# Weights decoded two chunks at a time, with loads, adds and the first batches placed anew, in an attention and FFN kernel

## Chip, cores and metric
One core of a Trainium2 chip. The metric is the device time of one execution in microseconds. All eight batches of an attention with memories and the FFN behind it run in one program; the host only lays arrays out.

## What is computed
Per batch and head, 32 memories gather keys and values of 576 positions with softmax weights over the heads' memory axis; queries attend to the 32 memories; the 4608 x 512 result goes through an FFN with a squared relu and d_ff = 2048. Inputs are fp32.

```
a = exp(phi - max(phi)); a = a / (sum(a) + 1e-9)
k_m = einsum('bhsm,bhsd->bhmd', a, k)
v_m = einsum('bhsm,bhsd->bhmd', a, v)
scores = q @ k_m.T / sqrt(64)
attn = exp(scores - max(scores)); attn = attn / (sum(attn) + 1e-9)
x = attn @ v_m, heads side by side
return square(relu(x @ w_in)) @ w_out
```

## The kernel before
**Names.** P = 128. A batch b has two tiles t of T = 288 tokens. d_ff is cut into 16 chunks f of 128. A *step* is one chunk f of one tile: `ffn1` (six matmuls on L566 into the PSUM tile h, relu on ScalarE at L568, the square at L572 on ScalarE or L574 on VectorE) and `ffn2` (matmuls into four accumulators). `ffn2` of a step runs two steps after its `ffn1` (LEAD). 256 steps, each cut into two *half steps*; steps of several tiles of batches 0 and 1 come in the order `runs` sets (tile (0,0), (0,1), (1,0) with chunks 0 to 3 first, then (1,1) with 0 to 7, ...).

**Attention folded into the FFN.** `attend` makes the softmax weights a of a tile over 4 x 2 heads x 32 memories, split into two fp32r parts a_hi and a_lo (L418, L419). `make_u` multiplies a unit n of w_in (512 columns of d_ff) with a batch's value memories, into the single PSUM tile ps_m, and splits it into u_hi (ScalarE, L456) and u_lo (VectorE, L458): unit (b,n). So `ffn1` is a @ u in three products: a_hi u_hi, a_hi u_lo, a_lo u_hi. `memories` also needs ps_m for every batch but the first.

**Weights.** w_in and w_out arrive as 64-bit words, in loads of 128 x 512 words (512 KB): w_in in 8 chunks of two halves, w_out in 16 chunks. `decode` turns a load into fp32: on ScalarE L479 (tile tmp) and L482 (tile low), on VectorE L484, L486 (mask and shift) and L489, then the add L496 on the engine that the plan names. `decode_out` then splits the chunk into two fp32r parts (L553 on ScalarE, L555 on VectorE); chunks 0 to 3 are first used whole in fp32 (L587, first 16 steps) and split later (`split_out`). Finished units of w_in are written to HBM (`keep_w`, L514) and streamed back for later batches. A load's tile is a `room` in the const pool; tmp has three buffers, low two.

**What sets the order.** The program is emitted in the order in which it should run; each engine takes its instructions in that order, and waits with everything behind. The start is written out: the list `loads` sets the order in which SP issues transfers (eight in flight), and the string `order` calls the generators of batch 0 (e exponentials, m memories, a0 and a1 the tiles' softmax, d0 to d3 the decodes of w_in chunks 0 and 1, u0 the first unit, s one filler matmul on ident). `spin` and `spin_r` are fillers whose results nobody reads; `spin_r` multiplies turn, a copy of e that L207 makes. After that the table `plan` gives each task of batches 0 to 2 and of the weights the half steps at which its parts are emitted; from batch 3 on a fixed pattern repeats. The dictionary in L945 drains some `ffn2` earlier than LEAD.

Of the kernel before, what the change touches and what calls it, by code (L numbers as in the profile page):

```python
# [24 lines left out]
def attn_moe_kernel(ctx: ExitStack, tc: tile.TileContext, qT, kv, phi, w_in, w_out, outT):  # L25
# [54 lines left out]
    def room(f, shape, dtype):  # L80
        return const.tile(shape, dtype, name=f"wo{f}")
# [97 lines left out]
    def exp_phi(b, e):  # L179
# [76 lines left out]
    def load_kv(b, qd, lent=None):  # L256

        got = []
        for c in range(NCH):
            if lent:  # L260
                t = lent(c)
            elif qd:

                name, bufs = ("tmp", 3) if c < 3 else ("low", 2)
                t = work.tile([P, 4, CW], F32, name=name, bufs=bufs)
            else:
                t = kvb[c]
                assert c not in kv_used
                kv_used.add(c)
# [106 lines left out]
    on_gpsimd = {(0, 0): (0, 1, 2), (0, 1): (0, 1, 2), (1, 0): (0, 1, 2), (1, 1): (0, 1), (2, 0): (1, 2), (2, 1): (0,)}  # L376

    def attend(b, t, q, mem, new_a):
# [18 lines left out]
        if starting:  # L397
            spin_r(*(turn[:, i:i + T] for i in (0, 1, 2, 4)))
# [65 lines left out]
    def fetch(src, f):  # L464
        raw = room(f, [P, src.shape[-1]], src.dtype)
        nc.sync.dma_start(out=raw, in_=src)
        return raw

    def decode(raw, new_out, adder):

        n = raw.shape[-1]

        def word(w, dtype):
            return raw.bitcast(dtype).rearrange("p (n w) -> p n w", w=2)[:, :, w]


        c = work.tile([P, n], I32, name="tmp", bufs=3)
# [3 lines left out]
        r = work.tile([P, n], I32, name="low", bufs=2)  # L481
# [17 lines left out]
    raws = {}  # L499
    w_in_at = {}  # L500


    lent = 2 * list(range(NFT - NQ * NFC, NFT))

    def fetch_w_in(n, qd):
        raws["in", n, qd] = fetch(w_in[n, qd], lent[NQ * n + qd])

    def fetch_w_out(f):
        raws["out", f] = fetch(w_out[f * P:(f + 1) * P], f)
# [7 lines left out]
    def decode_in(n, qd, adder=nc.gpsimd):  # L517

        def new_out():
            if n // 2 not in w_in_at:  # L520
                w_in_at[n // 2] = new_w()
            return w_in_at[n // 2][:, 2 * qd:2 * qd + 2, n % 2 * HC:n % 2 * HC + HC]

        yield from decode(raws.pop(("in", n, qd)), new_out, adder)
        ready.add(("in", n, qd))
# [7 lines left out]
    def decode_out(f, adder=nc.gpsimd, whole=False):  # L533

        def new_out():
            wo[f] = room(f, [P, DM], F32)
            return wo[f]

        w = yield from decode(raws.pop(("out", f)), new_out if whole else None, adder)
        if not whole:  # L540
            yield
            yield from split(f, w)
        ready.add(("out", f))

    def split_out(f):
        w = work.tile([P, DM], F32, name="tmp", bufs=3)
        nc.scalar.copy(w, wo[f])
        yield from split(f, w)

    def split(f, w):  # L550
        ready.discard(("out", f))
        wo[f] = room(f, [P, 2, DM], F32R)
        nc.scalar.copy(wo[f][:, 0], w)  # L553
        yield
        nc.vector.tensor_tensor(out=wo[f][:, 1], in0=w, in1=wo[f][:, 0].bitcast(F32), op=ALU.subtract)  # L555
        ready.add(("out", f))
# [68 lines left out]
    def new_mem(b):  # L625
        state[b]["mem"] = work.tile([P, 2, NPAIR, M], F32, name="mem", bufs=3)
# [44 lines left out]
    SQ_ACT = 39  # L671
# [52 lines left out]
    def next_kv():  # L724
# [36 lines left out]
    turn = const.tile([P, 3 * NQ * P], F32R, name=f"wo{NFT - 1}")  # L761
# [13 lines left out]
        "e e e e e m m d0 m m d0 s d0 a0 a0 a1 d1 d1 a0 a0 d1 u0 d2 a0 d2 u0 a0 u0 d3 d3 d2 s d3 s d3 a0"  # L775
# [11 lines left out]
    for n in kept:  # L787
# [5 lines left out]
        ((29, 29, 31), decode_in, 4, 0, nc.gpsimd),  # L793
        ((48, 53, 54), decode_in, 6, 0, nc.gpsimd),
        ((61,), task_kv, 2, 0),
        ((0, 1, 1), decode_out, 0, nc.gpsimd, True),
        ((6, 8, 10), decode_out, 3, nc.gpsimd, True),
        ((38, 43, 45), decode_in, 4, 1, nc.vector),
        ((110, 115), split_out, 0),
        ((5,), task_q, 1, 1),  # L800
        ((20,), fetch_w_in, 6, 1),
        ((90,), task_kv, 2, 1),
        ((0, 0, 2, 2, 3, 4), lambda: start["a1"]),
        ((50,), fetch_w_in, 7, 1),
        ((78, 81), split_out, 1),
        ((0, 1, 2), decode_out, 1, nc.gpsimd, True),
        ((47, 47, 49), decode_in, 6, 1, nc.vector),
        ((38,), fetch_w_out, 10),
        ((8,), fetch_w_in, 5, 0),
        ((62, 62, 64), decode_in, 7, 0, nc.vector),  # L810
        ((58, 59, 60), decode_in, 7, 1, nc.gpsimd),
        ((90,), task_stream, 2, 0),
        ((45, 46, 46, 48, 48), decode_out, 8, nc.vector),
        ((73, 73, 74), task_u, 0, 3),
        ((100, 101, 101, 102, 104, 107, 108), task_attend, 2, 0),
        ((52,), fetch_w_out, 13),
# [179 lines left out]
```

## Time and profile before

| | us |
|---|---|
| median of 3 runs | 739.28 |
| lowest, highest | 738.86, 742.27 |
| profiled execution | 739.42 |
| its span, first to last instruction | 737.6 |
| TensorE busy | 721.2 |
| VectorE, ScalarE, GpSimd busy | 379.6, 351.6, 263.8 |

The span is one execution on the core; 1.8 us lie around it. Times in the rows count from the span's start. TensorE's busy time is modelled at its ends, so a pause shorter than a matmul's tail does not show as idle; its weight loads (PEld) have rows of their own. A wait for several semaphores is put down to the one that came last.

### The profile page before, as it was taken

The page shows a single profiled execution, that of the slowest core. Times are in us where ns is not written, and L with a number is a line of the kernel's source. Part 1 is how long each engine was busy: PE and PEld are TensorE (multiplying, and loading weights), DVE is VectorE, ACT ScalarE, POOL GpSimd, SP SyncE. Part 2 cuts the span into 40 slices and gives each one's busy share as a digit, 9 for nine tenths or more (in the row PEclk, how much of TensorE's full clock was granted, in tenths as well). Part 3 has the DMA queues.
Part 4 walks back from the last instruction along what each step waited for, and adds up shares of the span by engine and source line. Part 5 has one row for each costly group of instructions (what it writes and reads, how often), then busy time and mean ns, then how long its engine had stood idle before and what let it go on. Part 6 is the DMA issues. An engine that isn't in the chain of part 4 may idle for free.

```text
span 737.6 us, 15709 instructions
## 1 busy us (share of the span) xinstructions
PE 721.2 (98%) x6170; PEld 655.1 (89%) x6170; DVE 379.6 (51%) x764; ACT 351.6 (48%) x750; POOL 263.8 (36%) x333
## 2 busy tenths in 40 slices
PE   8889999999999999999999999999999999999997
PEld 4467789889899898999899999899889999999997
DVE  4986779974565455254543556254542555321211
ACT  3546878874543344343544345433443435443332
POOL 1433334353443234332433324242333333333332
PEclk9999999999999999999999999999999999999999
DMA  9993228414429019131481216530391314100000
GB/s 306 354 363 117 105 67 265 147 30 125 140 76 313 25 56 298 44 122 34 143 222 44 80 33 244 122 121 2 87 281 31 122 34 147 58 33 1 33 2 32
DMA packets 64409, 89.61 MB, mean 121 GB/s; under 512 B 3984, under 2 KB 54928, under 8 KB 60752
## 3 DMA queue, kind: packets, MB, share of 16 engines
q1 hardware_dynamic: 63344, 87.34, 37.0%
q10 hardware_dynamic: 992, 1.28, 0.5%
q8 instruction: 48, 0.79, 0.4%
q14 instruction: 25, 0.20, 0.1%
HBM read 74.97 MB, written 13.63 MB: 120 GB/s over the span
## 4 chain that ended last, share of the span: by engine, by line
PE 83%; DVE 10%; ACT 4%; issue 1%; DMA 1%; POOL 1%; ACTq 0%; DVEq 0%; POOLq 0%
PE acc L595 49%; PE h L566 24%; PE ps_m L372 5%; PE ps_m L303 2%; DVE tmp L486 2%; DVE tmp L489 2%; PE acc L587 1%; DVE tmp L484 1%; DMA e_sb<-in_phi 1%; ACT low L482 1%; DVE u_lo L458 1%; ACT tmp L479 1%; DVE tmp L496 1%; ACT g L572 1%; ACT r L568 1%
## 5 line engine op out<-in xcount | busy, mean ns | idle before, releaser
L579 POOL TENSOR_TENSOR g_lo<-g,g_hi 128x288 fp32r<-128x288 f32 x240 | 202.4, 845 | 405.2 <-DVE g L574 313.3
L595 PE MATMUL acc<-g_hi,wo 128*128 128x288 f32 x1920 | 307.3, 298 | 0.4 <-DVE o L607 0.3
L595 PEld LDWEIGHTS acc<-g_hi,wo 128*128 128x128 f32 x1920 | 271.6, 188 | 25.3 <-ACT r L568 18.3
L574 DVE TENSOR_TENSOR g<-h,r 128x288 f32<-128x288 f32 x217 | 98.7, 456 | 307.3 <-ACT r L568 301.5
L568 ACT ACTIVATE r<-h 128x288 f32<-128x288 f32 x256 | 104.9, 410 | 295.0 <-PE h L566 286.4
L595 PE MATMUL acc<-g_lo,wo 128*128 128x288 f32 x960 | 176.5, 295 | 0.6 <-POOL g_lo L579 0.6
L595 PEld LDWEIGHTS acc<-g_lo,wo 128*128 128x128 f32 x960 | 144.2, 188 | 0.9 <-POOL g_lo L579 0.9
L577 ACT ACTIVATE g_hi<-r 128x288 fp32r<-128x288 f32 x240 | 106.5, 444 | 19.8 <-ACT r L568 0.8
L566 PE MATMUL h<-a_hi,u_hi 128*128 128x288 f32 x512 | 114.5, 305 | 0.7 <-ACT r L568 0.7
L566 PE MATMUL h<-a_hi,u_lo 128*128 128x288 f32 x512 | 109.8, 296 | 0.3 <-DVE u_lo L458 0.3
L566 PE MATMUL h<-a_lo,u_hi 128*128 128x288 f32 x512 | 109.6, 295 | 0.0
L566 PEld LDWEIGHTS h<-a_hi,u_hi 128*128 128x128 f32 x512 | 82.7, 188 | 10.5 <-issue 6.1
L566 PEld LDWEIGHTS h<-a_hi,u_lo 128*128 128x128 f32 x512 | 82.1, 188 | 0.5 <-DVE u_lo L458 0.5
L566 PEld LDWEIGHTS h<-a_lo,u_hi 128*128 128x128 f32 x512 | 82.2, 189 | 0.0
L458 DVE TENSOR_TENSOR u_lo<-ps_m,u_hi 128x1024 fp32r<-128x1024 f32 (+1 forms) x33 | 38.8, 1176 | 11.8 <-ACT u_hi L456 11.7
L372 PE MATMUL ps_m<-w_sb,mem 64*32 64x512 f32 (+1 forms) x528 | 37.1, 588 | 1.3 <-DVE w_sb L496 0.9
L587 PE MATMUL acc<-g_hi,wo 128*128 128x288 f32 x128 | 34.5, 414 | 1.7 <-POOL wo L496 1.7
L456 ACT CAST u_hi<-ps_m 128x1024 fp32r<-128x1024 f32 (+1 forms) x33 | 32.3, 980 | 5.0 <-PE ps_m L372 3.0
L587 PEld LDWEIGHTS acc<-g_hi,wo 128*128 128x128 f32 x128 | 23.6, 193 | 10.3 <-POOL wo L496 2.5
L482 ACT ACTIVATE low<-wo 128x512 int32<-128x512 uint32 x32 | 21.6, 674 | 8.6 <-DVE w_sb L496 4.4
L489 DVE SCALAR_TENSOR_TENSOR tmp<-wo,tmp 128x512 int32<-128x512 int32 x32 | 24.4, 761 | 1.1
L479 ACT ACTIVATE tmp<-wo 128x512 f32<-128x512 f32 x32 | 21.5, 672 | 4.4 <-DMA wo<-in_w_in 2.7
(136 smaller groups left out, 485.1 us busy)
## 6 DMA issues: line engine op xcount, KB each, us to landing
w_sb<-w_f SPq DMA_DIRECT2D x24, 1024.0 KB, 5.7
out_t<-o SPq DMA_DIRECT2D x62, 144.0 KB, 1.9
wo<-in_w_in SPq DMA_DIRECT2D x16, 512.0 KB, 8.3
wo<-in_w_out SPq DMA_DIRECT2D x16, 512.0 KB, 6.7
q_sb<-in_q SPq DMA_DIRECT2D x28, 288.0 KB, 3.4
kvb<-in_kv SPq DMA_DIRECT2D x28, 256.0 KB, 6.6
tmp<-in_kv SPq DMA_DIRECT2D x18, 256.0 KB, 6.0
w_f<-w_sb SPq DMA_DIRECT2D x4, 1024.0 KB, 7.6
```

Of the source, the lines that this page charges most:

```text
L372: nc.tensor.matmul(bank(out, half)[M * pr:M * (pr + 1), :y.shape[-1]], mem[hs, x, pr], y, start=True, stop=True)
L456: nc.scalar.copy(u_hi[:, :, n0:n1], ps[:, :, :n1 - n0])
L458: nc.vector.tensor_tensor(out=u_lo[:, :, n0:n1], in0=ps[:, :, :n1 - n0], in1=u_hi[:, :, n0:n1].bitcast(F32), op=ALU.subtract)
L482: nc.scalar.activation(r, word(0, U32), AF.Copy, scale=2.0 ** -29)
L489: nc.vector.scalar_tensor_tensor(out=c, in0=word(1, I32), scalar=-0x40000000, in1=c, op0=ALU.bitwise_and, op1=ALU.bitwise_or)
L566: nc.tensor.matmul(h[:, :T], u[:, qd, fs], x[:, qd], start=(i == 0), stop=(i == len(todo) - 1))
L568: nc.scalar.activation(r, h[:, :T], AF.Relu)
L574: nc.vector.tensor_tensor(out=g, in0=h[:, :T], in1=r, op=ALU.mult)
L577: nc.scalar.activation(g_hi, r, AF.Square)
L579: nc.gpsimd.tensor_tensor(out=g_lo, in0=g, in1=g_hi.bitcast(F32), op=ALU.subtract)
L587: nc.tensor.matmul(acc[e][:, :T], wo[f][:, e * P:(e + 1) * P], g_hi, start=first, stop=last)
L595: nc.tensor.matmul(acc[e][:, :T], wo[f][:, w, e * P:(e + 1) * P], x, start=first and x is g_hi and w == 0, stop=last and x is g_lo,)
```

## The change
`fetch` puts two loads of 512 KB side by side in one room, and `decode`, `decode_out` and `split` work on both at once, 128 x 1024; only w_in chunk 0 is still decoded by halves. The wide tmp has two buffers, the wide low one. Most adds are placed on VectorE: w_out pair 2 and w_in chunk 5 alone, and the two halves of w_in chunk 0, stay on GpSimd. Of the attention steps of batches 1 and 2 six of the operations 0 (subtract the maximum), 1 (multiply by the reciprocal) and 2 (a_lo) come from GpSimd to VectorE on balance. `spin_r` and the copy turn go; the start has plain fillers instead. SQ_ACT, the step up to which ScalarE makes the square, goes from 39 to 43. `loads`, `order`, `plan` and the early drains are new tables throughout.

```diff
-    def room(f, shape, dtype):
-        return const.tile(shape, dtype, name=f"wo{f}")
+    def room(k, shape, dtype):
+        return const.tile(shape, dtype, name=f"wp{k}")
...
-            nc.scalar.copy(turn.rearrange("p (c x) -> p c x", c=3), e_sb[:, :3])
...
-    on_gpsimd = {(0, 0): (0, 1, 2), (0, 1): (0, 1, 2), (1, 0): (0, 1, 2), (1, 1): (0, 1), (2, 0): (1, 2), (2, 1): (0,)}
+    on_gpsimd = {(0, 0): (0, 1, 2), (0, 1): (0, 1, 2), (1, 0): (), (1, 1): (), (2, 0): (2,), (2, 1): (2,)}
...
-            spin_r(*(turn[:, i:i + T] for i in (0, 1, 2, 4)))
+            spin(2, ident)
...
-    def fetch(src, f):
-        raw = room(f, [P, src.shape[-1]], src.dtype)
-        nc.sync.dma_start(out=raw, in_=src)
-        return raw
+    def fetch(src, key, k, i):
+        if key not in raws:
+            raws[key] = room(k, [P, 2, src.shape[-1]], src.dtype)
+        nc.sync.dma_start(out=raws[key][:, i], in_=src)
+        fetched.add((*key, i))
...
-        c = work.tile([P, n], I32, name="tmp", bufs=3)
+        c = work.tile([P, 2 * DM], I32, name="tmp", bufs=2)[:, :n]
...
-        r = work.tile([P, n], I32, name="low", bufs=2)
+        r = work.tile([P, 2 * DM], I32, name="low", bufs=1)[:, :n]
...
+    def split(k, w):
+        ready.difference_update(("out", 2 * k + i) for i in range(2))
+        y = room(k, [P, 2, 2, DM], F32R)
+        wo[2 * k:2 * k + 2] = [y[:, 0], y[:, 1]]
+        nc.scalar.copy(y[:, :, 0], w)
+        yield
+        nc.vector.tensor_tensor(out=y[:, :, 1], in0=w, in1=y[:, :, 0].bitcast(F32), op=ALU.subtract)
...
-    SQ_ACT = 39
+    SQ_ACT = 43
...
     loads = [
         (first_phi,),
         (first_kv, 0),
+        (task_q, 0, 1),
         (first_kv, 1),
-        (fetch_w_in, 0, 1),
         (fetch_w_in, 0, 0),
         (task_q, 0, 0),
-        (task_q, 0, 1),
+        (fetch_w_in, 0, 1),
         (fetch_w_in, 1, 0),
         (fetch_w_in, 1, 1),
+        (fetch_w_out, 2),
+        (next_kv,),
+        (fetch_w_in, 3, 1),
+        (fetch_w_out, 4),
         (fetch_w_out, 0),
         (fetch_w_out, 1),
...
-        ((0, 1, 1), decode_out, 0, nc.gpsimd, True),
-        ((0, 1, 2), decode_out, 1, nc.gpsimd, True),
+        ((0, 0, 0), decode_out, 0, nc.vector, True),
...
-        ((136, 142, 142), task_u, 2, 3),
-        ((109,), task_stream, 2, 3),
+        ((129, 134, 136), task_u, 2, 3),
+        ((112,), task_stream, 2, 3),
...
-        for _ in range({2: 1, 6: 1, 7: 1, 10: 1}.get(k, 0)):
+        for _ in range({2: 1, 7: 1, 8: 1, 9: 1}.get(k, 0)):
```

How the order moves at three places (line numbers in the second block of each are those of the changed file; names are out<-in with the shape of the output).

VectorE at the start, from the sum of tile (0,0)'s softmax to the u_lo of the first unit. Before:

```order
L406 TENSOR_REDUCE sm<-st 128x18
L407 TENSOR_SCALAR sm<-sm 128x18
L408 RECIPROCAL sm<-sm 128x18
L484 TENSOR_SCALAR tmp<-tmp 128x512
L486 TENSOR_SCALAR tmp<-tmp 128x512
L489 SCALAR_TENSOR_TENSOR tmp<-wo_129,tmp 128x512
L415 STREAM_TRANSPOSE at<-st 128x576
L458 TENSOR_TENSOR u_lo_333<-ps_m,u_hi_332 128x2x256
```

Now:

```order
L400 TENSOR_REDUCE sm<-st 128x18
L401 TENSOR_SCALAR sm<-sm 128x18
L402 RECIPROCAL sm<-sm 128x18
L478 TENSOR_SCALAR tmp<-tmp 128x1024
L480 TENSOR_SCALAR tmp<-tmp 128x1024
L483 SCALAR_TENSOR_TENSOR tmp<-wp_127,tmp 128x1024
L408 STREAM_TRANSPOSE at<-st 128x576
L490 ISA w_sb<-tmp,low 128x4x512
L451 TENSOR_TENSOR u_lo_344<-ps_m,u_hi_343 128x2x256
```

The decode of w_in chunk 1 between the reciprocal and the transpose is twice as wide, and its add stands ahead of u_lo.

ScalarE from the first FFN product's relu on. wo_133 and wo_391 are loads of w_out chunks 0 and 1; wp_373 is the room of both. Before:

```order
L568 ACTIVATE r<-h 128x288
L572 ACTIVATE g_hi<-r 128x288
L479 ACTIVATE tmp<-wo_133 128x512
L482 ACTIVATE low<-wo_133 128x512
L479 ACTIVATE tmp<-wo_391 128x512
L482 ACTIVATE low<-wo_391 128x512
L568 ACTIVATE r<-h 128x288
L572 ACTIVATE g_hi<-r 128x288
```

Now:

```order
L567 ACTIVATE r<-h 128x288
L571 ACTIVATE g_hi<-r 128x288
L473 ACTIVATE tmp<-wp_373 128x1024
L476 ACTIVATE low<-wp_373 128x1024
L449 CAST u_hi_343<-ps_m 128x2x256
L567 ACTIVATE r<-h 128x288
L571 ACTIVATE g_hi<-r 128x288
```

Four operations on halves become two on a pair, and the second half of the first unit's u_hi now stands behind them.

VectorE around the memories of batch 3, where u_lo of unit (2,3) frees ps_m and den is the first to read the memories. Before:

```order
L245 TENSOR_TENSOR e_sb<-e_sb,phi_mx 128x1024
L248 TENSOR_TENSOR e_sb<-e_sb,phi_mx 64x256
L574 TENSOR_TENSOR g<-h,r 128x288 x2
L458 TENSOR_TENSOR u_lo_3012<-ps_m,u_hi_3011 128x1024
L574 TENSOR_TENSOR g<-h,r 128x288
L312 TENSOR_SCALAR den<-ps_m 128x2
```

Now:

```order
L573 TENSOR_TENSOR g<-h,r 128x288 x2
L451 TENSOR_TENSOR u_lo_2704<-ps_m,u_hi_2703 128x1024
L224 STREAM_TRANSPOSE at<-phi_mx 128x256
L226 TENSOR_REDUCE top<-at 128x8
L229 TENSOR_TENSOR top<-top 32x8 x3
L231 COPY top<-top 32x8 x3
L573 TENSOR_TENSOR g<-h,r 128x288
L233 COPY at<-top 128x256
L234 STREAM_TRANSPOSE phi_mx<-at 128x256
L237 TENSOR_TENSOR e_sb<-e_sb,phi_mx 128x1024
L240 TENSOR_TENSOR e_sb<-e_sb,phi_mx 64x256
```

u_lo has moved ahead of all of batch 3's exponentials but their first maximum.

## Rows read from the trace of the kernel before

**Rows 1.** Section 1 of the page: busy time, share of the span and instructions of each engine.
```profile
PE 721.2 (98%) x6170; PEld 655.1 (89%) x6170; DVE 379.6 (51%) x764; ACT 351.6 (48%) x750; POOL 263.8 (36%) x333
```

**Rows 2.** Busy time by stretches; per engine busy us (x instructions), clock, DMA share, GB/s.
```profile
28.06:60.00 31.94, 26.65 (x261) 18.75 (x259) 25.86 (x42) 17.93 (x35) 11.73 (x10) 0.95 0.96 331
60.00:100.00 40.00, 39.35 (x233) 31.95 (x232) 30.00 (x46) 30.16 (x65) 15.05 (x12) 1.00 0.22 80
100.00:148.00 48.00, 47.35 (x377) 42.45 (x375) 41.96 (x64) 39.13 (x89) 19.91 (x20) 1.00 0.56 182
148.00:246.00 98.00, 95.95 (x872) 88.83 (x876) 57.76 (x113) 49.76 (x103) 39.08 (x54) 1.00 0.44 133
```

**Rows 3.** The chain of waits from 60 to 150 us, by line.
```profile
by line: DVE tmp L489 12.2%; DVE tmp L486 10.9%; DVE tmp L484 7.9%; ACT low L482 5.5%; ACT tmp L479 5.2%; issue 5.0%; DVE tmp L496 4.8%; ACT g L572 4.8%; ACT g_hi L577 4.3%; ACT r L568 4.1%; ACT wo L553 3.7%; DVE wo L555 3.4%; POOL tmp L496
```

**Rows 4.** The timeline before the first FFN product: start, us, engine, line [idle before <-releaser].
```profile
15.24 0.67 ACT L479 ACTIVATE tmp<-wo 128x512 f32<-128x512 f32 x1 [2.69 <-DMA wo<-in_w_in]
...
16.40 0.43 DVE L486 TENSOR_SCALAR tmp<-tmp 128x512 int32<-128x512 int32 x1
...
23.76 1.27 DVE L486 TENSOR_SCALAR tmp<-tmp 128x512 int32<-128x512 int32 x1
```

**Rows 5.** The timeline from the first FFN product to the third ffn2.
```profile
28.99 0.43 PE L566 MATMUL h<-a_lo,u_hi 128*128 128x288 f32 x2
...
36.26 2.21 PE L587 MATMUL acc<-g_hi,wo 128*128 128x288 f32 x8 [1.69 <-POOL wo L496]
...
40.28 1.37 DVE L174 TENSOR_TENSOR phi_mx<-at 128x256 f32<-128x256 f32 x1
...
42.15 0.57 PE L187 MATMUL ps_m<-ident,phi_mx 128*128 128x128 f32 x2 [2.37 <-DVE phi_mx L176]
...
48.27 1.50 DVE L484 TENSOR_SCALAR tmp<-tmp 128x512 f32<-128x512 f32 x1
...
50.80 2.21 PE L587 MATMUL acc<-g_hi,wo 128*128 128x288 f32 x8
```

**Rows 6.** Groups of one shape: xcount, busy us, mean ns, idle before; VectorE, ScalarE, then GpSimd.
```profile
L489 DVE SCALAR_TENSOR_TENSOR tmp<-wo,tmp 128x512 int32<-128x512 int32 x32 | 24.4, 761 | 1.1
L486 DVE TENSOR_SCALAR tmp<-tmp 128x512 int32<-128x512 int32 x32 | 22.3, 698 | 1.1
L484 DVE TENSOR_SCALAR tmp<-tmp 128x512 f32<-128x512 f32 x32 | 17.7, 554 | 1.1 <-ACT tmp L479 0.9
...
L412 DVE TENSOR_TENSOR st<-st,sm 128x576 f32<-128x576 f32 x11 | 8.3, 758 | 0.4
...
L496 DVE CUSTOM_DVE_ANT_0 w_sb<-tmp,low 128x1024 uint16<-128x1024 uint16 x9 | 7.2, 813 | 0.3
...
L210 DVE TENSOR_TENSOR e_sb<-e_sb,ps_m 128x1024 f32<-128x1024 f32 x2 | 2.4, 1217 | 1.9 <-PE ps_m L195 1.9
...
L479 ACT ACTIVATE tmp<-wo 128x512 f32<-128x512 f32 x32 | 21.5, 672 | 4.4 <-DMA wo<-in_w_in 2.7 <-DVE wo L555 1.7
...
L251 ACT ACTIVATE e_sb<-e_sb 128x1024 f32<-128x1024 f32 x5 | 5.2, 1044 | 0.0
...
L496 POOL TENSOR_TENSOR w_sb<-tmp,low 128x512 int32<-128x512 int32 x7 | 9.9, 1410 | 24.0 <-ACT tmp L479 14.2 <-ACT r L568 5.9 <-ACT o L614 2.7
```

**Rows 7.** DMAs issued at 4.8 to 5.0 and 26.2 to 26.4 us: KB each, us to landing.
```profile
wo<-in_kv SPq DMA_DIRECT2D x1, 128.0 KB, 7.8
...
wo<-in_w_out SPq DMA_DIRECT2D x1, 512.0 KB, 6.9
```

**Rows 8.** The stretch with the slow TensorE clock, columns as in rows 2.
```profile
42.30:45.70 3.40, 3.40 (x14) 3.19 (x14) 1.53 (x3) 1.52 (x3) 1.41 (x1) 0.50 1.06 391
```

**Rows 9.** The timeline at three waits of TensorE and ScalarE.
```profile
99.54 0.40 PE L566 MATMUL h<-a_hi,u_hi 128*128 128x288 f32 x1 [0.65 <-ACT r L568]
...
103.43 0.68 ACT L482 ACTIVATE low<-wo 128x512 int32<-128x512 uint32 x1 [1.40 <-DVE w_sb L496]
...
244.72 1.32 PE L303 MATMUL ps_m<-kvb,e_sb 128*32 128x130 f32 x40 [1.60 <-DVE u_lo L458]
```

More of the change, by code (lines that the diff above doesn't have):

```diff
@@ L262, in load_kv @@
             elif qd:
-                name, bufs = ("tmp", 3) if c < 3 else ("low", 2)
-                t = work.tile([P, 4, CW], F32, name=name, bufs=bufs)
+                if not c % 2:
+                    name, bufs = ("tmp", 2) if c // 2 < 2 else ("low", 1)
+                    pairs.append(work.tile([P, 2, 4, CW], F32, name=name, bufs=bufs))
+                t = pairs[-1][:, c % 2]
             else:
@@ L499, in attn_moe_kernel @@
     raws = {}
+    fetched = set()
     w_in_at = {}
-    lent = 2 * list(range(NFT - NQ * NFC, NFT))
     def fetch_w_in(n, qd):
-        raws["in", n, qd] = fetch(w_in[n, qd], lent[NQ * n + qd])
+        fetch(w_in[n, qd], ("in", n), NFT // 4 + n % (NFT // 4), qd)
     def fetch_w_out(f):
-        raws["out", f] = fetch(w_out[f * P:(f + 1) * P], f)
+        fetch(w_out[f * P:(f + 1) * P], ("out", f // 2), f // 2, f % 2)
     kept = []
@@ L521, in new_out @@
                 w_in_at[n // 2] = new_w()
-            return w_in_at[n // 2][:, 2 * qd:2 * qd + 2, n % 2 * HC:n % 2 * HC + HC]
-        yield from decode(raws.pop(("in", n, qd)), new_out, adder)
-        ready.add(("in", n, qd))
+            return w_in_at[n // 2][:, 2 * q0:2 * q1, n % 2 * HC:n % 2 * HC + HC]
+        assert all(("in", n, qd) in fetched for qd in range(q0, q1))
+        yield from decode(raws["in", n][:, q0:q1], new_out, adder)
+        ready.update(("in", n, qd) for qd in range(q0, q1))
         if all(("in", n ^ i, x) in ready for i in range(2) for x in range(NQ)):
@@ L531, in decode_in, with decode_out, split_out @@
             keep_w(n // 2)
[L533 removed]
+    def decode_out(k, adder=nc.gpsimd, whole=False):
         def new_out():
[L536 to L539 removed]
+            w = room(k, [P, 2, DM], F32)
+            wo[2 * k:2 * k + 2] = [w[:, 0], w[:, 1]]
+            return w
+        assert all(("out", k, i) in fetched for i in range(2))
+        w = yield from decode(raws.pop(("out", k)), new_out if whole else None, adder)
         if not whole:
             yield
[L542 to L553, printed above, removed]
+            yield from split(k, w.rearrange("p (i x) -> p i x", i=2))
+        ready.update(("out", 2 * k + i) for i in range(2))
+    def split_out(k):
+        w = work.tile([P, 2 * DM], F32, name="tmp", bufs=2).rearrange("p (i x) -> p i x", i=2)
+        for i in range(2):
+            nc.scalar.copy(w[:, i], wo[2 * k + i])
+        yield from split(k, w)
+    def split(k, w):
[3 more added lines that the diff above has]
+        nc.scalar.copy(y[:, :, 0], w)
         yield
[L555 to L556 removed]
+        nc.vector.tensor_tensor(out=y[:, :, 1], in0=w, in1=y[:, :, 0].bitcast(F32), op=ALU.subtract)
+        ready.update(("out", 2 * k + i) for i in range(2))
     def ffn1(f, u, a, square, whole):
@@ L877, in attn_moe_kernel @@
         at(places, fn, *args)
-    whole = {args[0] for _, fn, *args in plan if fn is decode_out and args[-1] is True}
+    whole = {2 * args[0] + i for _, fn, *args in plan if fn is decode_out and args[-1] is True for i in range(2)}
     for b in range(3, B):
```

184 lines of the change are left out of this document (80 added, 104 removed).

## The prediction

> **What bounds the kernel now.** I read the page first, then the stretches, then the chain of waits, then the timeline of the first 60 us. TensorE is busy for 721.2 of 737.6 us [rows 1], so nothing but TensorE's own pauses can be won. The stretches [rows 2] say where they are: 31.94 - 26.65 = 5.3 us idle between the first FFN product (28.06 us) and 60 us, 0.65 us up to 100, 0.65 us up to 148, 2.05 us up to 246, and next to none from there to the last drain. The change alters nothing behind step 71, so the stages up to 246 us are all it can reach; the 28 us before the first FFN product are the other part. Between 60 and 150 us the chain of waits runs mostly through VectorE's decode lines L484, L486 and L489 and ScalarE's L479 and L482 [rows 3]: TensorE is nearly full there, but only just fed by these two. VectorE is busy for 25.9 of 31.9, 30.0 of 40 and 42.0 of 48 us [rows 2].
>
> **The start, up to the first FFN product.** DMA order: q of tile (0,1), 576 KB, now stands ahead of the second half of K/V. At the stretch's 331 GB/s [rows 2] that is 1.8 us later for a transfer that was issued at 4.9 us and landed after 7.8 us [rows 7], so 14.5 instead of 12.7 us. Much of it is covered: before, the first w_in chunk held ScalarE until it landed at 15.2 us [rows 4], and it keeps its place but for 64 KB. The other chunk, which had landed early, now comes about 1,660 KB later. Bounds 0 and 1.8 us; I take +0.6, since ScalarE's wait for the first chunk sets most of it as before. Then the decode of w_in chunk pair 1 stands between the sum of the softmax and the transpose at L415, now 1,024 wide. The price of a wide operation is not in the trace for tensor_scalar: a free 512-wide L486 took 0.43 us [rows 4], so 1,024 lies between 0.43 and 0.86; I take 0.65. For L489 and the add L496 I take 1.22 us, what a two-input 128x1024 operation took (L210 [rows 6]), though its bounds reach from 0.7 to 1.4, once and twice the 512-wide ones. The same L486 took 1.27 us at 23.76 us [rows 4], because GpSimd's multiply ran: it ended just after it, and a wide one will too. So the three operations take some 3.1 us (bounds 2.2, as now, and 4.4) instead of 2.2: +0.9. The transpose, the cast and a_lo behind it, and with a_lo the third pair of the first FFN product (28.99 us [rows 5]), come about 0.6 + 0.9 = 1.5 us later. The matmuls on the turned copy of e (L148) and the copy itself (L207) go, and plain fillers on ident come in their place; all of them fill waits, so that is nothing by itself.
>
> **From there to the third ffn2.** The first ffn2 (36.26 us [rows 5]) waited for w_out chunk 0, decoded with its add on GpSimd. Now chunks 0 and 1 must both have landed. By bytes ahead of it (9,792 KB) chunk 1 stands within 64 KB of the load issued in 26.2 to 26.4 us, which landed after 6.9 us [rows 7]: 33.2 us. ScalarE's first wide operation takes about 1.1 us (512 wide 0.67, 1,024 wide from SBUF 1.04 [rows 6]; the strided read is the dearer one), then VectorE 0.65 + 0.65 + 1.22 + 1.22 = 3.7 us: 38.0 us, 1.7 us later than before. It comes back: from the first to the third ffn2 (36.26 to 50.80 us) VectorE was held up by GpSimd's decode adds, for instance L174, 1.37 us at 40.28, and L484, 1.50 us at 48.27 [rows 5], each 0.43 at most when free, as the 512-wide one of 16.40 us [rows 4]. The adds of w_out pairs 0 and 1 are now VectorE's, so 2.0 us of stretching go in these two, and I put 0.2 on the smaller ones: 38.0 + 14.54 - 2.2 = 50.3, that is **-0.5 us** (bounds -2 and +2). SP's list of loads holds the same 15,680 KB, so its last one, now half of w_in chunk pair 3, lands when its last one did, near 50 us by 331 GB/s and the time in flight. ScalarE waits for it there, with batch 1's copy of the memories queued behind; those memories are done at about the same time, so this wait costs nothing, and if it grows, the scores of tile (1,0) are late next.
>
> **From there to 148 us.** VectorE's three decode operations cost 32 x (0.554 + 0.698 + 0.761) = 64.4 us [rows 6]. Now there are 15 pairs and two single chunks: 15 x 2.52 + 2 x 1.55 = 41 us without stretching, some 47 with a third of it left. Adds on VectorE: 16 x 0.81 = 13 us become 13 x 1.22 = 16. Six of attention's 128x576 operations in batches 1 and 2 come over from GpSimd, 6 x 0.76 = +4.6 [rows 6]; four squares (steps 39 to 42) go to ScalarE, about -1.8. Net about -12 us of VectorE's 98 us up to 148. ScalarE: 64 x 0.67 = 43 become 4 x 0.67 + 30 x 1.1 = 36 us. GpSimd keeps four of its sixteen adds of some 1.4 us, two of them now wide. Both engines that fed TensorE thus get air. What it can give is TensorE's idle time there, 0.65 + 0.65 = **-1.3 us**; I take all of it. Its pauses were ScalarE's (0.65 us at 99.54, where relu came late [rows 9]).
> [...]
>
> **From 148 to 246 us.** At 244.72 us TensorE waited 1.60 us for the u_lo of unit (2,3), whose PSUM tile batch 3's memories need [rows 9]. Its three parts stand at half steps 136, 142, 142 and the memories at 143; now at 129, 134, 136. That leaves 7 half steps, and its weights are streamed in at half step 112: **-1.6 us** (bounds 0 and -2.05).
>
> **Sum.** The profiled execution took 739.42 us: 739.4 - 0.5 - 1.3 - 1.6 = **736.0 us**. The median before is 739.28, so it stands for the same. A measurement of this kernel tells some 0.5%, 3.7 us, from no change: faster means under 735.6, slower over 743.0.
>
> **Rivals.** *The clock* (chance 0.2): TensorE ran at half its clock from 42.3 to 45.7 us (0.50, 1.2 GHz [rows 8]), after waits of 1.69 and 2.37 us at L587 and L187 [rows 5]. Now one filler stands ahead of the first ffn2 instead of two, and the wait there is about 4 us (from some 34 to 38). If two such stretches follow and one lies where TensorE is what is waited for, half of 3.4 us is lost there, 1.7 us, and the 0.5 of the start as well, and what is late passes on to batch 1's attention: 736.0 + 0.5 + 1.7 + 1 = 739.2. Against it: VectorE is what is waited for until about 47 us, which hides a slow TensorE. [...]
> *One buffer for low* (0.15; slower): the second operand of a decode had two tiles and now has one, so ScalarE's L482 waits for the add of the pair before, and relu and the squares of the FFN stand behind it. Already with two tiles it waited 1.40 us at 103.43 [rows 9], and ScalarE's two wide operations take 2.2 instead of 1.35 us. It decides once such a wait exceeds about 1 us, the air that 1.3 us of relu and squares leave in a step of 2.4 us. Ten pairs at 0.65 us each, the stall at 99.54 [rows 9], and the 1.3 not won: 736.0 + 6.5 + 1.3 = 743.8. Against it: the adds that release the tile are no longer queued on a held-up VectorE.
> *The start gains too* (0.15): K/V is covered whole (0 of 0.6), VectorE's relief takes away half the 5.3 us idle before 60 us: 736.0 - 0.6 - 2.6 = 732.8.
> *It doesn't do what it says at 244 us* (0.05): something else than the PSUM tile, such as batch 3's exponentials on the same half steps, keeps the memories back: 737.6.
> **How the numbers follow.** My case has 0.45, its own range 733.5 to 738.5. Faster than 735.6: two fifths of it, 0.18, the better start, 0.15, and 0.03 of the rest: 0.36. Slower than 743.0: most of the buffer rival and a little of the clock's: 0.13. The rest, 0.51, is the same. Range 732.0 to 742.5: it leaves out the worse half of the buffer rival and the outer ends of the better start, about 0.2.
>
> **What would show it.** First FFN product ends near 30.9 us, first ffn2 at 38, third near 50; the granted clock of 36 to 46 us tells the clock rival. The wide mask-and-shift (L486 before) near 0.65 to 0.8 us in the mean; GpSimd's decode adds four. ScalarE's waits for low under 1 us. No pause before the memories of batch 3. I am wrong if TensorE's idle time between 60 and 148 us grows, or the first ffn2 comes after 40 us.

## The result, and the profile after

The changed kernel takes 730.11 us (median; 729.51 to 730.82) against 739.15 of the kernel before beside it: ratio 0.9869, interval 0.9841 to 0.9896. That is 9.0 us faster where 3.3 were forecast, below the range of 732.0 to 742.5 and below the fastest rival, 732.8. The profiled execution took 730.05 us, its span is 728.3.

The first section of the page, after (busy time, share, instructions), answers to [rows 1]:

```profile
PE 715.7 (98%) x6154; PEld 649.0 (89%) x6154; DVE 366.8 (50%) x710; ACT 348.8 (48%) x715; POOL 248.0 (34%) x315
```

The stretches, after, cut as in [rows 2], with the same columns:

```profile
28.06:60.00 31.94, 27.68 (x270) 20.12 (x269) 26.43 (x40) 20.08 (x35) 5.54 (x4) 0.95 0.87 300
60.00:100.00 40.00, 40.00 (x254) 32.56 (x254) 29.43 (x35) 31.25 (x58) 7.17 (x6) 1.00 0.37 132
100.00:148.00 48.00, 47.66 (x387) 43.30 (x386) 35.17 (x39) 39.42 (x75) 21.46 (x19) 1.00 0.55 180
148.00:246.00 98.00, 97.83 (x912) 91.77 (x911) 56.05 (x113) 46.60 (x98) 36.94 (x50) 1.00 0.39 123
```

TensorE idles 0 + 0.34 + 0.17 us from 60 to 246 us, where it idled 0.65 + 0.65 + 2.05. That is 2.8 us of the 9. The rest is not idle time at all, so I went by marks: the first matmul of each batch's memories. They stand at the same place in both programs. TensorE's timeline, before, then after; batch 3's row before is in [rows 9]:

```profile
48.10 0.32 PE L303 MATMUL ps_m<-kvb,e_sb 128*32 128x130 f32 x4
...
172.07 0.32 PE L303 MATMUL ps_m<-kvb,e_sb 128*32 128x130 f32 x4
...
330.43 0.32 PE L303 MATMUL ps_m<-kvb,e_sb 128*32 128x130 f32 x4
...
587.52 0.32 PE L303 MATMUL ps_m<-kvb,e_sb 128*32 128x130 f32 x4
```

```profile
46.52 0.32 PE L297 MATMUL ps_m<-kvb,e_sb 128*32 128x130 f32 x4
...
166.98 0.32 PE L297 MATMUL ps_m<-kvb,e_sb 128*32 128x130 f32 x4
...
237.81 0.32 PE L297 MATMUL ps_m<-kvb,e_sb 128*32 128x130 f32 x4
...
323.08 0.31 PE L297 MATMUL ps_m<-kvb,e_sb 128*32 128x130 f32 x3
...
579.00 0.32 PE L297 MATMUL ps_m<-kvb,e_sb 128*32 128x130 f32 x4
```

| stretch | before | after | difference | forecast |
|---|---|---|---|---|
| start to batch 1's memories | 48.10 | 46.52 | -1.58 | -0.5 |
| to batch 2's | 123.97 | 120.46 | -3.51 | -1.3 |
| to batch 3's | 72.65 | 70.83 | -1.82 | -1.6 |
| to the end of the span | 492.9 | 490.4 | -2.5 | 0 |

The last line is the surprise: tasks and order are the same there, TensorE is full in both, and yet a batch takes (587.52 - 330.43) / 3 = 85.70 us before and (579.00 - 323.08) / 3 = 85.31 after.

### The profile page after: what moved, and what is told of

Same layout as the page of the kernel before. It is cut to its first block, busy times and chain, and to the rows that moved or that the text cites. A ratio compares the mean times of both kernels' runs of the same rounds, so it can differ in the third digit from the quotient of the medians.

```text
span 728.3 us, 15552 instructions
## 1 busy us (share of the span) xinstructions
PE 715.7 (98%) x6154; PEld 649.0 (89%) x6154; DVE 366.8 (50%) x710; ACT 348.8 (48%) x715; POOL 248.0 (34%) x315
## 4 chain that ended last, share of the span: by engine, by line
PE 90%; DMA 5%; ACT 2%; DVE 2%; issue 0%; SPq 0%; ACTq 0%; DVEq 0%
PE acc L594 51%; PE h L565 27%; PE ps_m L366 5%; PE acc L586 4%; PE ps_m L297 2%; DMA u_hi<-in_kv 1%; DMA wp<-in_w_out 1%; DMA wp<-in_kv 1%; DMA w_sb<-w_f 1%; DMA e_sb<-in_phi 1%; DVE tmp L483 0%; DVE wp L490 0%; ACT r L567 0%; ACT low L476 0%; ACT tmp L473 0%
## 5 line engine op out<-in xcount | busy, mean ns | idle before, releaser
L578 POOL TENSOR_TENSOR g_lo<-g,g_hi 128x288 fp32r<-128x288 f32 x240 | 207.9, 867 | 408.7 <-DVE g L573 289.9
L594 PE MATMUL acc<-g_hi,wp 128*128 128x288 f32 x1920 | 304.1, 296 | 0.3 <-ACT g_hi L576 0.3
L594 PEld LDWEIGHTS acc<-g_hi,wp 128*128 128x128 f32 x1920 | 269.3, 188 | 19.8 <-ACT r L567 15.7
L573 DVE TENSOR_TENSOR g<-h,r 128x288 f32<-128x288 f32 x213 | 96.7, 456 | 305.8 <-ACT r L567 299.0
L594 PE MATMUL acc<-g_lo,wp 128*128 128x288 f32 x960 | 175.9, 295 | 0.0
L594 PEld LDWEIGHTS acc<-g_lo,wp 128*128 128x128 f32 x960 | 144.1, 188 | 0.0
L586 PE MATMUL acc<-g_hi,wp 128*128 128x288 f32 x128 | 35.2, 420 | 4.2 <-DVE wp L490 4.1
L366 PE MATMUL ps_m<-w_sb,mem 64*32 64x512 f32 (+1 forms) x528 | 35.1, 588 | 0.3 <-DVE st L387 0.2
L586 PEld LDWEIGHTS acc<-g_hi,wp 128*128 128x128 f32 x128 | 23.7, 193 | 12.6 <-DVE wp L490 5.3
L473 ACT ACTIVATE tmp<-wp 128x1024 f32<-128x1024 f32 (+1 forms) x17 | 18.5, 1087 | 9.4 <-DMA wp<-in_w_in 8.2
L412 POOL TENSOR_TENSOR a_lo<-at,a_hi 128x576 fp32r<-128x576 f32 x14 | 20.4, 1454 | 6.8 <-ACT a_hi L411 6.8
L483 DVE SCALAR_TENSOR_TENSOR tmp<-wp,tmp 128x1024 int32<-128x1024 int32 (+1 forms) x17 | 20.3, 1195 | 0.6
```

The costliest lines, as they stand in the source:

```text
L366: nc.tensor.matmul(bank(out, half)[M * pr:M * (pr + 1), :y.shape[-1]], mem[hs, x, pr], y, start=True, stop=True)
L412: by(2).tensor_tensor(out=a_lo, in0=at, in1=a_hi.bitcast(F32), op=ALU.subtract)
L483: nc.vector.scalar_tensor_tensor(out=c, in0=word(1, I32), scalar=-0x40000000, in1=c, op0=ALU.bitwise_and, op1=ALU.bitwise_or)
L573: nc.vector.tensor_tensor(out=g, in0=h[:, :T], in1=r, op=ALU.mult)
L578: nc.gpsimd.tensor_tensor(out=g_lo, in0=g, in1=g_hi.bitcast(F32), op=ALU.subtract)
L586: nc.tensor.matmul(acc[e][:, :T], wo[f][:, e * P:(e + 1) * P], g_hi, start=first, stop=last)
```

## The experiments

The kernel before was run again beside each set of experiments, with medians of 739.15 to 740.57 us. Whole times of different sets can therefore be compared to about 1 us only; below that the marks in the traces decide.

### Why the untouched part became faster (e1, e2)

Theory A: widening the tiles tmp and low moved every tile of the work pool behind them. In the built programs g_hi and g_lo start 96 bytes past a multiple of 128 before the change, and on a multiple of 128 after it. In both kernels I put one unused tile of 32 bytes a partition ahead of r. In the built programs r, g_hi, g and g_lo move by these 32 bytes, and with them what lies behind: q_sb and the small tiles of the attention (phi_mx, st, mx, sm, at, top). The weights, a and u stay, and so does the order:

```diff
     def ffn1(f, u, a, square, whole):
+        if not padded:
+            padded.append(work.tile([P, 8], F32, name="pad", bufs=1))
+            nc.gpsimd.memset(padded[0], 0.0)
```

> The changed kernel, with one unused tile of 32 bytes a partition made ahead of r, so that r, g_hi, g and g_lo start 32 bytes past a multiple of 64 as they did before the change, and nothing else moves. Theory A (where the moving operand starts sets the pace of the 12 ffn2 matmuls): from batch 3 on the matmul-to-matmul time goes from some 132.3 ns back to 133.4, the period of a batch from 85.27 to 85.7 us, and the whole from 730.1 to 733.3 us (240 steps x 12 x 1.1 ns = 3.2). Theory B (the changed order of tasks lets TensorE run denser): no change, 730.1 us, period 85.3.

> The kernel before, with the same unused tile of 32 bytes: r, g_hi, g and g_lo now start at multiples of 64 bytes. Theory A: the period of a batch from batch 3 on falls from 85.7 to 85.3 us and the whole from 739.1 to 735.9 us. Theory B: 739.1 us, period 85.7.

The kernel before gained: 736.92 us against 740.05 beside it, ratio 0.9959 (0.9946 to 0.9972), that is -3.0 us (-4.0 to -2.1). Its batches are now as short as those of the changed kernel, (588.18 - 332.22) / 3 = 85.32 us. TensorE's timeline of e2:

```profile
332.22 0.32 PE L303 MATMUL ps_m<-kvb,e_sb 128*32 128x130 f32 x4
...
588.18 0.31 PE L303 MATMUL ps_m<-kvb,e_sb 128*32 128x130 f32 x3
```

Theory B is out: the order did not change, and the gain came. So the layout is the cause, but which of the moved tiles counts these two runs don't separate. e1 lost only 1.5 us (731.57, ratio 0.989, 0.9873 to 0.9906), half of what A expected. "32 past a multiple of 64" was therefore not the rule. Hence more places.

### Which place (e8 to e12)

e8, e10 and e11 take the same edit with 96, 64 and 128 bytes. e9 lays the six tiles alternately. e12 moves the constant tiles too, the weights among them, and has 192 bytes ahead of r:

```diff
-        g_hi = work.tile([P, T], F32 if whole else F32R, name="g_hi", bufs=3)
+        g_hi = new_g("g_hi", F32 if whole else F32R)
...
-        g_lo = work.tile([P, T], F32R, name="g_lo", bufs=3)
+        g_lo = new_g("g_lo", F32R)
```

```diff
+    apart = const.tile([P, 16], F32, name="apart")
+    nc.gpsimd.memset(apart, 0.0)
     e_sb = const.tile([P, NCH, NQ * P], F32, name="e_sb")
```

> The changed kernel with an unused tile of 96 bytes a partition ahead of r: g_hi and g_lo start 96 past a multiple of 128, as before the change (with 32 bytes it was 32 past). Read by the mean time from matmul to matmul in ffn2 from batch 3 on. If the place within 128 bytes sets the pace: 133.4 ns (132.25 at 0, 132.41 at 32). If what matters is something else in the layout of before: 132.2 to 132.5.

> The changed kernel with the six tiles of g_hi and g_lo laid alternately (g_hi0, g_lo0, g_hi1, ...), so that every g_hi starts 128 and every g_lo 0 past a multiple of 256, as the best of the three pairs does now (its steps run at 131.5 ns from matmul to matmul, the others at 132.5 and 132.7). Theory G (the place within 256 bytes sets the pace): all steps at 131.5 ns, the whole 2.1 us shorter (240 x 12 x 0.75 ns), 728.0 us. Theory H (only the place within 128 matters, the three paces come from something else): mean 132.2, the whole 730.1 us.

> The changed kernel with an unused tile of 64 bytes a partition ahead of r: g at 64 past a multiple of 128. Read by the pace of ffn2 from batch 3 on. If the pace grows with the place (132.25 ns at 0, 132.41 at 32, 133.29 at 96): some 132.8. If only 96 is bad: 132.2 to 132.5.

> The changed kernel with an unused tile of 128 bytes a partition ahead of r. If the place within 128 bytes decides alone: the same three paces, mean 132.25 ns. Theory G, the place within 256 bytes: the steps that have both tiles at 0 and both at 128 keep 132.5 and 132.7 but change places among the three, and the third pair, now reversed, has a pace of its own other than 131.5.

> The changed kernel with unused tiles of 64 bytes ahead of all its constant tiles and of 192 ahead of r: the weights, u, a and the rest move by 64 bytes (from 64 to 0 past a multiple of 128), g by 256, so that its place within 256 stays. If the place of the weights matters as that of g does: the pace of ffn2 leaves 132.25 ns by more than 0.3, up or down, some 1 us or more in the whole. If only the operand that streams past matters: 132.1 to 132.4, 730.1 us, and ffn1's pace, whose streaming operand a moved, may change.

The paces are means from start to start of neighbouring matmuls, from 250 us on: of matmuls 2 to 12 of a step's ffn2, and 2 to 6 of its ffn1, worked out from the starts in each trace.

| kernel | g past a multiple of 128 | ffn2 ns | ffn1 ns | whole us |
|---|---|---|---|---|
| before | 96 | 133.38 | 132.29 | 739.15 |
| e2: before, +32 | 0 | 132.25 | 131.72 | 736.92 |
| after | 0 | 132.25 | 131.72 | 730.11 |
| e1: after, +32 | 32 | 132.41 | 132.54 | 731.57 |
| e10: after, +64 | 64 | 132.60 | 132.28 | 731.28, one run |
| e8: after, +96 | 96 | 133.29 | 133.47 | 734.93, one run |
| e11: after, +128 | 0 | 132.37 | 132.39 | 732.04, one run |
| e9: alternate | 0 | 132.02 | 132.75 | 731.00 |
| e12: constants +64, g +256 | 0 | 132.58 | 131.74 | 731.07 |

e8 agrees, by its trace: the changed kernel with g at 96 is as slow per batch as the kernel before, (582.82 - 325.23) / 3 = 85.86 us:

```profile
325.23 0.32 PE L297 MATMUL ps_m<-kvb,e_sb 128*32 128x130 f32 x4
...
582.82 0.32 PE L297 MATMUL ps_m<-kvb,e_sb 128*32 128x130 f32 x4
```

From before to after, a step of 12 + 6 matmuls is 12 x 1.13 + 6 x 0.57 = 17 ns shorter, 4.1 us over the 240 split steps; e2 measured 3.0, with an interval that reaches 4.0. e1's loss follows from its paces too: (12 x 0.16 + 6 x 0.82) ns x 240 = 1.6 us, most of it in ffn1.

The rule stays open. G and H both fall: alternate tiles gave 132.0 everywhere, not 131.5, and ffn1 became slower. Since e9 moves g_hi, g and g_lo alone, their place does count. The place within 128 bytes does not decide alone, as e11's ffn1 is 0.67 ns slower, and e10's 132.60 lies between its two cases. ffn1's pace moved with g although its own operands a and u had not, and it stayed at 131.74 in e12, where they had: it is not simply the operand that streams past. e12 stands 0.33 ns above the changed kernel in ffn2, just past the bound that its expectation set, but more than the weights moved in it, so whether their place counts stays open. The changed kernel has the shortest step of those tried; no rearrangement beat it.

### The pause ahead of batch 3's memories (e3)

```diff
-        ((129, 134, 136), task_u, 2, 3),
+        ((136, 142, 142), task_u, 2, 3),
```

> The changed kernel with unit (2,3) back at half steps 136, 142, 142. If the PSUM tile is what kept batch 3's memories back, a pause of about 1.6 us returns ahead of them: 731.7 us. Rival, the exponentials of batch 3 or the denser VectorE kept them back: under 0.5 us, 730.1 to 730.6.

732.11 us, 2.0 above the changed kernel, and the pause is back in TensorE's timeline, ended by the same u_lo as in [rows 9]:

```profile
240.87 0.32 PE L297 MATMUL ps_m<-kvb,e_sb 128*32 128x130 f32 x4 [1.62 <-DVE u_lo L451]
```

The rival is out: the unit that held the PSUM tile was the cause, and 1.6 us its price.

### What won the stretch between the memories of batches 1 and 2 (e4 to e7, e13)

The expectations of e5, e6, e7 and e13, and the table below, count this stretch from the last piece of batch 1's memories, 1.5 us later than the rows above: 122.5 us before, 118.9 after. That of e4 counts from the first.

e4, width alone: each wide operation in two halves, back to back.

```diff
-        nc.scalar.activation(size, word(1, F32), AF.Abs)
+        for s in halves:
+            nc.scalar.activation(size[:, s], word(1, F32)[:, s], AF.Abs)
...
```

> The changed kernel with each operation of decode and of split on a pair issued as two of 128x512, back to back, at the same places and on the same engines. Theory C (the width is what relieved VectorE and ScalarE): a pair costs VectorE 2 x (0.55 + 0.70 + 0.76 + 0.81) = 5.6 us instead of 4.1, up to 1.5 x 15 = 23 us in all, and the time from batch 1's to batch 2's memories, 120.5 us, goes most of the way back to the 123.4 that remain of 124.0 without the alignment's 0.5: the whole 732.5 to 733.5 us. Theory D (the new order and the adds that left GpSimd gave it, the width little): under 0.7 us slower, 730.1 to 730.8.

730.14 us, the stretch 118.5: nothing is lost. Yet the width does save VectorE time. Groups of one shape (count, busy us, mean ns, idle before), after, then e4, where L491, L482 and L486 are the lines L483, L478 and L480 of after:

```profile
L483 DVE SCALAR_TENSOR_TENSOR tmp<-wp,tmp 128x1024 int32<-128x1024 int32 x15 | 18.9, 1262 | 0.5
...
L480 DVE TENSOR_SCALAR tmp<-tmp 128x1024 int32<-128x1024 int32 x15 | 11.7, 782 | 0.5
L478 DVE TENSOR_SCALAR tmp<-tmp 128x1024 f32<-128x1024 f32 x15 | 11.0, 731 | 10.3 <-ACT tmp L473 10.2
...
L490 POOL TENSOR_TENSOR w_sb<-tmp,low 128x1024 int32<-128x1024 int32 x1 | 2.4, 2407 | 0.0
```

```profile
L491 DVE SCALAR_TENSOR_TENSOR tmp<-wp,tmp 128x512 int32<-128x512 int32 x32 | 21.2, 701 | 0.1
L482 DVE TENSOR_SCALAR tmp<-tmp 128x512 f32<-128x512 f32 x32 | 14.4, 478 | 9.5 <-ACT tmp L475 9.2
L486 DVE TENSOR_SCALAR tmp<-tmp 128x512 int32<-128x512 int32 x32 | 13.6, 463 | 0.1
```

Two halves cost 2 x (701 + 478 + 463) = 3284 ns, a pair 1262 + 731 + 782 = 2775: 0.17 us saved per operation in the mean, and 2 x 701 - 1262 = 140 ns for the two-input one. It buys no time here. Most of the shrinkage against [rows 6] is not width either: at the same 512, L486 fell from 698 to 463 ns and L484 from 554 to 478.

e5 puts five adds back on GpSimd, e6 the attention operations, and e7 gives the kernel before the tile of e2, the place of unit (2,3), and the new engines:

```diff
-        ((0, 0, 0), decode_out, 0, nc.vector, True),
+        ((0, 0, 0), decode_out, 0, nc.gpsimd, True),
...
```

```diff
-(1, 0): (), (1, 1): (), (2, 0): (2,), (2, 1): (2,)}
+(1, 0): (0, 1, 2), (1, 1): (0, 1), (2, 0): (1, 2), (2, 1): (0,)}
```

The last, against the kernel before, with the tile of e2 and the attention engines of after besides:

```diff
-        ((136, 142, 142), task_u, 2, 3),
+        ((129, 134, 136), task_u, 2, 3),
...
-        ((0, 1, 1), decode_out, 0, nc.gpsimd, True),
+        ((0, 1, 1), decode_out, 0, nc.vector, True),
...
```

> The changed kernel with the adds of w_out pairs 0, 1 and 7 and of w_in chunks 2 and 4 put on GpSimd, so that 16 of the 512-wide adds' worth run there, as before the change. Theory E (GpSimd's adds stretch VectorE's operations and come late; moving them is what won the stretch from batch 1's to batch 2's memories): first ffn2 about 1 us later, the wide mask-and-shift above 0.9 us in the mean, and that stretch grows from 118.9 to over 120.5 us; the whole 732 us or more. Theory F (the order of the tasks in the table won it): stretch within 0.7 us of 118.9, the whole 730 to 731.

> The changed kernel with the attention operations of batches 1 and 2 on GpSimd and VectorE as before the change. Theory E: the softmax of batches 1 and 2 stretches VectorE and comes later; the stretch between the memories of batches 1 and 2 grows by 0.5 to 1.5 us, the whole 730.6 to 731.6. Theory F: under 0.3 us.

> The kernel before, with its 512-wide decodes and its order, with the unused tile of 32 bytes, unit (2,3) at half steps 129, 134, 136, the attention operations on the engines of the changed kernel, and all decode adds of the table on VectorE but those of w_out chunks 4 and 5. The tile (about -3.1) and the unit (about -1.7) alone give some 734.5 us. Theory E: the stretch between the memories of batches 1 and 2 falls from 122.5 to 123.2 us to under 121, the whole to 732 or 733. Theory F: the stretch stays at 122 to 123.5 us, the whole at 734 to 735.

| kernel | order | width | adds on GpSimd, in 512s | stretch | whole |
|---|---|---|---|---|---|
| before | old | 512 | 16 | 122.5 | 739.15 |
| e2: tile | old | 512 | 16 | 123.2 | 736.92 |
| e7: tile, unit, engines | old | 512 | 4 | 121.8 | 733.80 |
| after | new | 1,024 | 6 | 118.9 | 730.11 |
| e4 | new | 512 | 6 | 118.5 | 730.14 |
| e6: attention put back | new | 1,024 | 6 | 118.8 | 731.16 |
| e5: adds put back | new | 1,024 | 16 | 121.9 | 735.15 |
| e13: adds put back | new | 512 | 16 | 119.5 | 731.34 |

e2's marks, TensorE's timeline:

```profile
50.67 0.28 PE L303 MATMUL ps_m<-u_hi,e_sb 128*32 128x128 f32 x1
...
173.91 0.32 PE L303 MATMUL ps_m<-kvb,e_sb 128*32 128x130 f32 x4
```

e6 leaves the stretch as it was, so the attention operations are not the reason; its whole is 1.0 us up, as theory E has it, but ahead of the stretch and within the scatter. e5 is 5 us slower, as theory E says. But e7 gains only 0.7 us (against before) to 1.4 us (against e2, with the same tile) in the stretch by the same move in the old order and stays over 121, where E expected less; F's 122 to 123.5 fails as well. Two of its three waits there are for what VectorE does late. TensorE's waits in that stretch, e7 (us, times, longest):

```profile
PE acc L601 <- DVE o L613: 1.0, 1, 1.0
PE ps_m L372 <- DVE u_lo L458: 0.7, 1, 0.7
PE acc L593 <- ACT o L620: 0.6, 1, 0.6
```

So the price in e5 needed another reason: the width of the adds. e13 is e4 and e5 in one.

> The changed kernel with both edits of before: every decode operation in two of 512 (no loss by itself, 730.14 us) and the same five adds on GpSimd (with wide adds: 735.15 us, the stretch between the memories of batches 1 and 2 121.9 us instead of 118.9). Theory J (it is the width that makes an add on GpSimd dear: 2.4 us at one go, which holds the one low tile and stretches VectorE): most of the 5 us goes, 731 to 732.5 us, stretch under 120.3. Theory K (any add on GpSimd at these places costs it): 734 to 735.5 us, stretch 121.3 or more.

Theory J holds: 731.34 us. A rest stays even with narrow adds: 0.8 us in the whole, at the edge of the scatter, against the changed kernel run beside it (e15, 730.53), and 0.6 us in the stretch. A wide add on GpSimd takes 2.4 to 2.7 us at one go and stretches VectorE's mask-and-shift to 918 ns (782 after, 444 per half in e13). It holds the only low tile, so ScalarE stands, with relu behind it. Groups of one shape in e5, and its timeline on ScalarE and GpSimd:

```profile
L490 POOL TENSOR_TENSOR w_sb<-tmp,low 128x1024 int32<-128x1024 int32 x3 | 8.0, 2678 | 24.5 <-DVE tmp L483 18.2 <-ACT tmp L473 6.3
...
L480 DVE TENSOR_SCALAR tmp<-tmp 128x1024 int32<-128x1024 int32 x15 | 13.8, 918 | 0.5
```

```profile
90.05 2.86 POOL L490 TENSOR_TENSOR w_sb<-tmp,low 128x1024 int32<-128x1024 int32 x1 [6.30 <-ACT tmp L473]
...
92.95 1.17 ACT L476 ACTIVATE low<-wp 128x1024 int32<-128x1024 uint32 x1 [2.98 <-POOL w_sb L490]
```

This is my rival of the single buffer. It did not come about, because the change took the wide adds off GpSimd: ScalarE's longest wait for low after the change is 1.21 us, a little over the 1 us that I gave as its sign:

```profile
87.65 1.20 ACT L476 ACTIVATE low<-wp 128x1024 int32<-128x1024 uint32 x1 [1.21 <-DVE w_sb L490]
```

The other part of e5's loss is at the start, where TensorE waited 4.9 us for the first ffn2, instead of 4.1. Its granted clock had a mean of 0.58 from 39 to 46 us, but runs without these adds fell as low (see the start, below):

```profile
39.00:46.00 7.00, 6.69 (x24) 5.53 (x25) 3.88 (x7) 2.11 (x4) 1.66 (x2) 0.58 1.03 373
```

What is left to explain the stretch is the order: new in e13 (119.5 us), old in e2 (123.2), at the same width, number of adds on GpSimd and place of g. The order stands here for all that came with it: the tables, the halves of a pair next to each other, the buffers of tmp and low, SQ_ACT and the early drains. The layout gives some 0.3 to 0.5 of the 3.5 between before and after (e8, with the old place of g, has 119.3; a batch of 85.7 us gained 0.39). Which part of the order does it was not tried.

### What remains (e14, e15)

In some profiles one batch was 0.5 to 1.1 us longer than its 85.2. e14 issues the streams of w_in two half steps earlier; e15 is the changed kernel again.

```diff
-            ((23,), task_stream, b, 0), ((29, 30, 31), task_u, b, 0),
+            ((21,), task_stream, b, 0), ((29, 30, 31), task_u, b, 0),
...
```

> The changed kernel with the four streams of each later batch's w_in units issued two half steps (some 2.4 us) earlier. In some profiles a batch's period was 0.5 to 1.1 us longer than its 85.2, once with TensorE waiting 0.8 us for such a stream. If these late streams are what remains there: every period at 85.2 to 85.3 us, median 0.3 to 1 us under the changed kernel beside it. Else the same median and the same odd periods.

> The changed kernel unaltered, beside the others on the same chip: 729.5 to 731 us, an odd period of 85.4 to 86.4 us now and then.

730.45 and 730.53 us, and no odd batch in either profile. Nothing was won. Whether late streams make the odd batches stays open. No run beat the changed kernel.

## Why the prediction was wrong

**The start: right in its marks, its size within the scatter.** The first FFN product ends at 31.2 us (30.9 forecast), the first ffn2 starts at 37.77 (38.0), the third at 49.45 (50.3, [rows 5]: 50.80). TensorE's timeline, after:

```profile
30.81 0.43 PE L565 MATMUL h<-a_lo,u_hi 128*128 128x288 f32 x2
...
37.77 3.25 PE L586 MATMUL acc<-g_hi,wp 128*128 128x288 f32 x8 [4.09 <-DVE wp L490]
...
49.45 2.21 PE L586 MATMUL acc<-g_hi,wp 128*128 128x288 f32 x8
```

The later w_out chunks and VectorE's chain came as worked out, and VectorE gave the time back. The gain at batch 1's memories is 1.58 us between these two profiles. Kernels with the same start reach that mark between 46.5 and 48.6 us, 47.4 in the mean of eleven profiles, against 48.1 and 49.2 in the two with the old start: 1.2 us, known to about 1. With adds off GpSimd the old start was early too, in e7's one profile: 46.76, with no stretch at half clock near it. The clock rival did not cost more than before in this profile, one stretch at half clock instead of one [rows 8]. In six of those eleven profiles it came about, with twice the length at half clock (e14 below); they reach the mark at 47.8 us in the mean, the other five at 46.9. That is a difference of 0.8 us, where I had priced the rival at 3.2, and it may be part of the scatter. After, then e14, columns as in [rows 2]:

```profile
39.00:41.00 2.00, 2.00 (x6) 1.41 (x5) 1.93 (x4) 0.00 (x0) 1.38 (x1) 0.50 1.07 361
```

```profile
37.00:43.00 6.00, 5.37 (x14) 4.22 (x15) 5.19 (x9) 1.55 (x2) 1.41 (x1) 0.50 1.07 329
```

The profile gives the clock as a share of full speed alone, and no run shows the 1.2 GHz of my forecast. What the trace shows is the pace at 0.50: in the stretch of [rows 8] matmuls of 288 columns started (43.49 - 43.01) / 2 = 0.24 us apart, where ffn1's mean before the change is 132.29 ns at 1.00. TensorE's timeline, before:

```profile
43.01 0.68 PE L566 MATMUL h<-a_hi,u_lo 128*128 128x288 f32 x2
...
43.49 0.68 PE L566 MATMUL h<-a_lo,u_hi 128*128 128x288 f32 x2
```

That TensorE's waits bring the half clock about was my guess; no run tests it.

**60 to 148 us: the term was mis-sized, and its reason was wrong.** The step that failed is "What it can give is TensorE's idle time there, 0.65 + 0.65". The same work between the marks, before, after, then e5 and e13, columns as in [rows 2]:

```profile
49.60:172.07 122.47, 120.69 (x909) 103.71 (x900) 97.08 (x155) 91.48 (x198) 49.71 (x51) 1.00 0.39 131
```

```profile
48.05:166.98 118.93, 118.42 (x908) 103.01 (x901) 87.86 (x108) 91.33 (x173) 39.05 (x38) 1.00 0.44 149
```

```profile
50.60:172.50 121.90, 119.08 (x907) 102.98 (x901) 87.70 (x104) 90.88 (x173) 47.14 (x42) 1.00 0.41 139
```

```profile
49.17:168.60 119.43, 118.55 (x907) 103.04 (x901) 90.41 (x154) 93.66 (x204) 46.64 (x48) 1.00 0.43 144
```

With 909 and 908 matmuls, TensorE's busy time itself fell by 2.3 us, and its idle time only by 1.78 - 0.51 = 1.3, the value of my term. Some 0.5 of the 2.3 is the layout. The rest are pauses that the view had booked as busy, since a matmul's end is modelled: from start to start of matmuls, the delays of over 0.25 us beyond the usual pace of their form add up to 6.0 us before and 3.6 after. I said that busy time is modelled in describing the profile and did not use it. As the cause I named relief of VectorE and ScalarE, by width and by fewer adds on GpSimd. ScalarE got none (91.48 and 91.33 us). VectorE got 9.2 of the 12 us forecast, but in e5 VectorE is as little busy (87.70 us), and hardly any of the gain is left. The width is worth nothing (e4). The adds matter chiefly because the width makes them dear: back on GpSimd they cost 3.0 us of the stretch when wide (e5), 0.6 when narrow (e13). The order is what remains, by elimination.

**148 to 246 us: right.** Forecast -1.6, measured -1.82, of which some 0.3 is layout by the gain of a batch; e3 shows the 1.62 us and its cause. The rival at this place falls.

**Behind 246 us: the step that failed is "The change alters nothing behind step 71, so the stages up to 246 us are all it can reach".** The instructions are the same, but their tiles moved, and each split step became 17 ns shorter. This is worth 3.0 us in the whole (e2). With it and the full pauses of the stretch before, the sum is -1.2 (start) - 3.0 - 1.6 - 3.0 = -8.8, against -9.0 measured. That it comes so close is luck: the start and the layout are each known to about 1 us.

## What to carry to other kernels

When a tile changes its size, what is allocated behind it moves, so compare the pace of matmuls in a stretch that the change doesn't touch, before crediting or blaming the schedule. What an engine can win in a stretch is read from the same work between the same two marks, not from its idle time. Make an operation wider only together with the question of which engine runs it: doubled, an add on GpSimd held a buffer for 2.4 to 2.7 us and stretched its neighbour, while on VectorE the width was harmless and, in this order, useless.

## What the runs showed of the hardware

The mean pace of fp32r matmuls of 288 columns at the granted clock of 1.00 lies between 131.7 and 133.5 ns, by where tiles stand: about 1% between the best and the worst place in ffn2 (132.02 and 133.38) and 1.3% in ffn1 (131.72 and 133.47). Why is open. It repeats to 0.01 ns: the three buffer pairs of g run at 131.54, 132.72 and 132.48 ns after the change, and at 131.55, 132.73 and 132.48 in e2, a different program with g at the same places modulo 1,024 bytes. GpSimd's add of 128x1024 integers took 2.4 to 2.7 us, and VectorE's 0.78 us mask-and-shift took 0.92 us in the mean when seven of them ran instead of two (e5).
